# Folding U by f32 products on TensorE, and the rows of batch 0 half by half, in a kernel of two transforms and a mixer

## The chip, the cores and the metric

The kernel runs on one core of a Trainium2 chip. The metric is the device time of one execution in microseconds (us). The engines are TensorE (PE; its weight loads are PEld), VectorE (DVE), ScalarE (ACT), GpSimd (POOL) and SyncE (SP); DMA queues are issued from SP, ACT and POOL.

## The reference, cut to what matters

x is 8 x 3136 x 256 (batch, row, feature). The real part of its Fourier transform over rows and features is mixed over the rows by a low-rank pair U (3136 x 32) and V, and goes through two products with a ReLU between:

```
X = np.fft.fft(np.fft.fft(x, axis=1), axis=2).real
h = X.transpose(0, 2, 1) @ U @ V
u = X + h.transpose(0, 2, 1)
out = u + np.maximum(u @ w_ch1, 0) @ w_ch2
```

## The kernel before, in words

The transform over the 3136 rows is a product with tables of sines (`tabs`) and cosines (`tabc`), in bf16. The symmetry of the tables makes the work a quarter: rows n and S-n, and n and n+1568, are first added or subtracted. So batch b's rows come twice, `xf` forward (a gather on POOL, `load_f`, L67) and `xr` backward (`load_r`, L71; for batch 0 on SP), each in two halves a = 0 and 1 of 98 partitions x 8 rows x 256 features of f32 (784 KB), plus one-row edges (`load_0f`, `load_0r`). VectorE then folds. `along_d` (L299) folds along the features: part 0 subtracts (columns 1 to 127), part 1 adds (129 to 255). `alone` (L306, POOL) copies the two columns without a partner. `mirror` (L310) joins xf and xr of one half into `eos`, and `half` (L314) adds and subtracts the two halves into `G[b][par]`, the stationary operand of the row transform. `fold` (L318) is this for batches 1 to 7, `load_half` (L86) asks for the next batch's half once it has been read.

`seq` (L332) is one group of the row transform: 8 matmuls (4 for the later type) of 98 x 425 columns into a PSUM bank. Two groups of one parity and type are a pair: ACT copies the first to `ev` (L355), VectorE joins it with the second (L358 to L369) into `tab`, `A` and `B`. In batch 0 the order is g1, g2 (parity 0, type 0), g3, g4 (parity 1, type 0), g5 to g8 (type 1, on the later columns). Three banks serve all "dft" tiles, so g4 takes the bank of g1 and g6 that of g2. `chan` (L461) does the transform along the features from `A`, `B` with `MC`, `MSN`, `lowrank` (L472) the products with U, `front` (L504) the low-rank correction for 512 rows, `first_product` (L524) and `second_product` (L534) the two big products, 49 chunks of 512 rows. The fold and transform of the batches 1 to 7 are dealt out among these by `due` (L704 to L736).

U's own transform is columns 393 to 424 of the tables. For that U is folded in the same manner as x: UF is turned in its order of partitions by an f32 product with an exchange matrix `fl` (`turn_u`, L194), VectorE adds or subtracts UR from PSUM (L204) and then the halves (L207) into `GU` (`fold_u`, L202). `transform_u` (L222) contracts it with the tables on PE (L232), ACT keeps it (L238), PE turns it (L245), ACT writes it into the tables (L250, L251). `us` is this for the sines, `uc` for the cosines.

All of the set-up, batch 0's transform and the first chunk stand in an order written by hand (a manual schedule, from L93 until chunk 1): each engine does its instructions in the order of the program text. Lines 586 to 702 are that order. The tables' phases are on VectorE (`phase`, L167, two instructions each), their sines on ACT, mirrored copies on POOL or ACT (`turned_copy`, L264). The phases `pd` of the feature transform (L662 to L668) stand on VectorE between the fold of the first columns and that of the later ones; ACT makes `MSN` and `MC` of them, ahead of the first `ev` copy in its queue. The rows of batch 1 are asked for on POOL at L673 to L685.

Of the kernel before, what the change touches and what calls it, by code (L numbers as in the profile page):

```python
# [10 lines left out]
BF16 = mybir.dt.bfloat16  # L11
FP32 = mybir.dt.float32
I32 = mybir.dt.int32
# [14 lines left out]
def kernel(  # L28
# [81 lines left out]
    lrow = gen.tile([P, 2, P], FP32, tag="lrow", name="lrow", bufs=1)  # L110
    pcol = gen.tile([P, 1], FP32, tag="pcol", name="pcol", bufs=1)
    load_0f(moe_U, UF, 0, R, nc.scalar)
    load_0r(moe_U, UR, 0, R, nc.scalar)
    for t, n0, step in ((UF, 1, HALF), (UR, S - 784, -HALF)):
        nc.sync.dma_start(out=t[:PQ].rearrange("p a i d -> p a (i d)"),
                          in_=bass.AP(moe_U.tensor, moe_U.offset + n0 * R,
                                      [[8 * R, PQ], [step * R, 2], [1, 8 * R]]))
    load_r(0, 0)
    load_0f(x, xf, 0, D, nc.sync)
    load_0r(x, xr, 0, D, nc.sync)  # L120
    load_r(0, 1)
    for a in range(2):
        load_f(0, a)
# [1 line left out]
                   allow_small_or_imprecise_dtypes=True)  # L125
    nc.gpsimd.iota(fl[:, 1], pattern=[[1, P]], base=0, channel_multiplier=-1,
                   allow_small_or_imprecise_dtypes=True)
    nc.gpsimd.iota(fsel[:], pattern=[[R, 2], [2 * R, 2], [1, R]], base=0, channel_multiplier=-1,
                   allow_small_or_imprecise_dtypes=True)
    nc.gpsimd.iota(lrow[:], pattern=[[0, 2], [1, P]], base=0, channel_multiplier=0,  # L130
# [57 lines left out]
    uo = gen.tile([KP, 2, NI, R], FP32, name="uo", bufs=1)  # L188
    ue = gen.tile([KP, 2, NI, R], FP32, name="ue", bufs=1)
    GU = [gen.tile([KP, 2, NI, R], BF16, name=f"gu{par}", tag=f"gu{par}", bufs=1) for par in range(2)]  # L190

    TURNED = []

    def turn_u():  # L194
        nc.vector.tensor_single_scalar(fl[:], fl[:], 0.0, op=AL.is_equal)
        nc.vector.tensor_copy(fl[:KP, 0, PQ:KP], fl[:KP, 1, PQ:KP])
        pf = psum.tile([KP, 2, NI, R], FP32, tag="dft", name="pf", bufs=3)
        nc.tensor.matmul(pf.rearrange("p a i r -> p (a i r)"), fl[:KP, 0, :KP],
                         UF.rearrange("p a i r -> p (a i r)"), start=True, stop=True)
        TURNED.append(pf)  # L200

    def fold_u(typ):  # L202
        h = (uo, ue)[typ]
        nc.vector.tensor_tensor(h[:], TURNED[0][:], UR[:, :, ::-1, :],  # L204
                                op=AL.subtract if typ == 0 else AL.add)
        for par in range(2):
            nc.vector.tensor_tensor(GU[par][:, typ], h[:, 0], h[:, 1],  # L207
                                    op=AL.add if par == 0 else AL.subtract)


    hv = cpool.tile([P, 1], FP32, name="hv")
    hw = cpool.tile([P, 1], FP32, name="hw")
# [6 lines left out]
    def kp(i):  # L219
        return KP if i == NI - 1 else PQ  # L220

    def transform_u(typ):  # L222

        t = {}

        def contract():
            acc = t["acc"] = psum.tile([P, NQ], FP32, tag="dft", name="pu", bufs=3)
            for n in range(NI // 2):
                for g in range(4):
                    pk, pn = divmod(g, 2)  # L230
                    i = ktiles(pk)[n]
                    nc.tensor.matmul(acc[g * R:(g + 1) * R, :], GU[pn][:kp(i), typ, i, :],  # L232
                                     tabs[typ][:kp(i), i, pn, :NQ],
                                     start=(n == 0), stop=(n == NI // 2 - 1))
# [351 lines left out]
    for m, i in ((0, 0), (1, 2)):  # L586
        odd_row(m, i)
    cosine_odd(2)
    for m, i in ((2, 4), (3, 6)):
        odd_row(m, i)  # L590
    cosine_odd(6)
    for m, i in enumerate((7, 5, 3, 1)):
        phase(phe[:, m], krow[:KP, :, NH - 1:], ncol[:KP, i:i + 1], 15)
        sine(tabs[0][:, i, :, NH - 1:NQ], phe[:, m], 15, 1)
        if m == 0:
            mirror_even(0, 7)
            turn_u()
# [13 lines left out]
    fold_u(1)  # L611
    us, uc = transform_u(0), transform_u(1)
    us[0]()
    cosine(tabs[1][:, 7, :, NH - 1:NQ], phe[:, 0], 15)
    mirror_even(1, 7)
    cosine(tabs[1][:, 3, :, NH - 1:NQ], phe[:, 2], 15)
    nc.scalar.copy(cells(1, 3, 0, 1, NH - 1, 1), cells(1, 3, NQ - 1, -1, NH - 1, 0))
    us[1]()
    us[2]()
    cosine_low(5)  # L620
    cosine_high(1)
    us[3]()
    for a in range(2):
        alone(a, xr, EOR_)
    nc.gpsimd.iota(pint[:], pattern=[[0, 1]], base=D, channel_multiplier=-1)
    nc.gpsimd.memset(pint[0:1], P)
    nc.gpsimd.dma_start(out=W1[:, 0, :], in_=moe_w_ch1[0:P, :])
    w1t = gen.tile([P, H], FP32, name="w1t", tag="w1t", bufs=1)
    gather(w1t[:], moe_w_ch1, D, pint[:], H, 0)
    for a in range(2):  # L630
        alone(a, xf, EOF_)
# [3 lines left out]
    column_zeros()  # L635
    for s in range(2):
        nc.gpsimd.memset(TA[s][:].bitcast(I32), 0)
        if s == 0:
            av = alt.rearrange("p (l two) -> p l two", two=2)
            nc.gpsimd.memset(av[:, :, 0:1], 1.0)  # L640
            nc.gpsimd.memset(av[:, :, 1:2], -1.0)
        nc.gpsimd.tensor_copy(TA[s][R:R + 2, :], alt[R:R + 2, :])
        nc.gpsimd.memset(TA[s][R:R + 1, :], 0.0)
        nc.gpsimd.memset(TA[s][R:R + 1, 0:1], 1.0)
        nc.gpsimd.memset(TA[s][R:R + 1, P:P + 1], -1.0)
    for par in range(2):
        nc.gpsimd.memset(G[1][par][:, :, 258:GW].bitcast(I32), 0)
    along_d(0, xr, EOR_, 0)
    along_d(1, xr, EOR_, 0)
    halve(1)  # L650
    for step in uc:
        step()
    for a in range(2):
# [4 lines left out]
    for a in range(2):  # L658
        mirror(a, slice(256, 258), AL.add)
    for par in range(2):  # L660
        half(0, par, slice(256, 258))
    nc.vector.memset(lrow[:, 1, 0:1], 128.0)  # L662
    nc.vector.tensor_single_scalar(pcol[:], pcol[:], 1.0 / D, op=AL.mult)
    pd = gen.tile([P, 2 * P], I32, name="pd", bufs=1)
# [6 lines left out]
    for a in range(2):  # L671
        along_d(a, xr, EOR_, 1)
    for a in range(2):  # L673
        load_r(1, a)
    load_0r(x, xr, 1, D, nc.gpsimd)
    for a in range(2):
        along_d(a, xf, EOF_, 1)
        mirror(a, slice(128, 256), AL.add)
    for par in range(2):
        half(0, par, slice(128, 256))  # L680
    nc.gpsimd.memset(msr[:, :, 0:1], 1.0)
    nc.gpsimd.memset(msr[:, :, 1:2], -1.0)
    for a in range(2):
        load_f(1, a)
    load_0f(x, xf, 1, D, nc.gpsimd)  # L685
    nc.gpsimd.tensor_copy(W1[:, 1, :], w1t[:])
    nc.gpsimd.memset(VA[1][:].bitcast(I32), 0)
    nc.gpsimd.dma_start(out=VA[1][:R, :], in_=moe_V)
    steps = list(transform(0))
# [77 lines left out]
```

## Time and profile before

| what | before |
|---|---|
| three runs, median (lowest to highest) | 486.08 us (485.12 to 487.95) |
| the profiled execution: time, span | 486.03 us, 484.3 us |
| PE busy, share of the span | 459.6 us, 95% |
| VectorE busy | 317.0 us, 65% |
| ScalarE busy | 280.9 us, 58% |
| GpSimd busy | 69.1 us, 14% |
| mean granted clock of PE | 0.992 |
| PE idle before its matmuls of g1, from 24 us on | 2.43 us, released by VectorE's g |

The profile is of one execution. Its page gives busy times by engine, the busy tenths in 40 slices of the span, the chain of work that ended last, and groups of instructions by line; the timeline lists instructions in order of time, with the idle time of the engine before them and what ended it. Times in it count from the span's start. A busy PE is not a PE at its peak rate: matmuls of one shape take twice as long in some stretches as in others.

### The profile page before, as it was taken

The page shows a single profiled execution, that of the slowest core. Times are in us where ns is not written, and L with a number is a line of the kernel's source. Part 1 is how long each engine was busy: PE and PEld are TensorE (multiplying, and loading weights), DVE is VectorE, ACT ScalarE, POOL GpSimd, SP SyncE. Part 2 cuts the span into 40 slices and gives each one's busy share as a digit, 9 for nine tenths or more (in the row PEclk, how much of TensorE's full clock was granted, in tenths as well). Part 3 has the DMA queues.
Part 4 walks back from the last instruction along what each step waited for, and adds up shares of the span by engine and source line. Part 5 has one row for each costly group of instructions (what it writes and reads, how often), then busy time and mean ns, then how long its engine had stood idle before and what let it go on. Part 6 is the DMA issues. An engine that isn't in the chain of part 4 may idle for free.

```text
span 484.3 us, 7936 instructions
## 1 busy us (share of the span) xinstructions
PE 459.6 (95%) x3003; PEld 289.1 (60%) x3003; DVE 317.0 (65%) x713; ACT 280.9 (58%) x532; POOL 69.1 (14%) x123
## 2 busy tenths in 40 slices
PE   1479999999999999999999999999999999999997
PEld 0234656665566666666666666666666666666665
DVE  8895979684669657776568657684678543434333
ACT  7525744765666556655566556655566556656562
POOL 5882321110022000130022001120000000000000
PEclk9997999999999999999999999999999999999999
DMA  7589798975276823793376725684324233343533
GB/s 187 140 171 217 164 214 165 135 187 138 65 181 184 211 66 108 187 229 93 91 193 172 187 65 144 185 206 106 88 66 117 80 85 91 87 106 97 126 89 129
DMA packets 103606, 67.24 MB, mean 139 GB/s; under 512 B 73546, under 2 KB 100068, under 8 KB 100416
## 3 DMA queue, kind: packets, MB, share of 16 engines
q1 hardware_dynamic: 97722, 40.70, 36.4%
q0 software_dynamic: 5824, 26.03, 19.9%
q8 instruction: 23, 0.38, 0.3%
q14 instruction: 15, 0.12, 0.1%
q10 hardware_dynamic: 22, 0.00, 0.0%
HBM read 29.33 MB, written 25.69 MB: 114 GB/s over the span
## 4 chain that ended last, share of the span: by engine, by line
PE 87%; DVE 7%; DMA 3%; issue 1%; SPq 1%; DVEq 0%
PE p L546 34%; PE p L530 33%; PE pt L351 10%; PE ph L510 4%; DMA xr<-in_x_dram 3%; PE pst L466 2%; PE pst L468 2%; PE ptt L478 1%; DVE eof L304 1%; DVE eof L302 1%; DVE u L518 1%; DVE eos L311 1%; DVE eor L304 1%; PE ptc L437 1%; DVE eor L302 0%
## 5 line engine op out<-in xcount | busy, mean ns | idle before, releaser
L532 ACT ACTIVATE h<-p 128x512 bf16<-128x512 f32 x392 | 224.7, 599 | 153.8 <-PE p L530 153.7
L530 PE MATMUL p<-u,w 128*128 128x512 bf16 x784 | 218.3, 379 | 0.4 <-DVE u L518 0.3
L546 PE MATMUL p<-w,h 128*128 128x256 bf16 x1568 | 203.1, 273 | 0.0
L546 PEld LDWEIGHTS <-h 128*128 128x128 bf16 x1568 | 153.1, 98 | 59.4 <-DVE o L555 0.3
L530 PEld LDWEIGHTS <-w 128*128 128x128 bf16 x784 | 75.5, 98 | 53.6 <-issue 2.7
L552 DVE TENSOR_TENSOR o<-p,ut 128x4 f32<-128x4 f32 (+1 forms) x100 | 16.4, 164 | 93.1 <-PE p L546 91.2
L351 PEld LDWEIGHTS <-g 98*128 98x128 bf16 (+1 forms) x288 | 28.8, 101 | 34.0 <-DVE g L315 5.1
L358 DVE TENSOR_TENSOR tab<-pt,ev 128x32 bf16<-128x32 f32 x32 | 6.0, 189 | 58.2 <-PE pt L351 58.2
L55 POOL DMA_INDIRECT xf<-in_x_dram,xidx x16 | 17.3, 1079 | 170.2 <-DVE eof L304 162.9
L554 DVE TENSOR_TENSOR o<-p,ut 128x254 f32<-128x254 f32 (+1 forms) x100 | 40.5, 405 | 0.0
L555 DVE TENSOR_TENSOR o<-p,ut 128x254 f32<-128x254 f32 (+1 forms) x100 | 40.5, 405 | 0.0
L351 PE MATMUL pt<-tabc,g 98*128 98x425 bf16 (+1 forms) x160 | 37.9, 366 | 2.5 <-DVE g L315 1.7
L518 DVE TENSOR_TENSOR u<-ph,S 128x512 bf16<-128x512 f32 (+15 forms) x64 | 34.9, 554 | 2.1 <-ACT S L470 2.1
L518 DVE TENSOR_TENSOR u<-ph,T 128x512 bf16<-128x512 f32 (+15 forms) x64 | 34.8, 554 | 0.0
L351 PE MATMUL pt<-tabs,g 98*128 98x425 bf16 (+1 forms) x128 | 29.6, 355 | 2.4 <-DVE g L315 2.4
L510 PE MATMUL ph<-va,ta 128*128 128x512 bf16 (+18 forms) x128 | 29.4, 329 | 0.0
L355 ACT COPY ev<-pt 128x425 f32<-128x425 f32 x32 | 16.4, 514 | 22.4 <-PE pt L351 16.9
L311 DVE TENSOR_TENSOR eos<-eof,eor 99x1024 bf16<-99x1024 bf16 (+2 forms) x34 | 21.9, 660 | 0.1
L466 PE MATMUL pst<-A,mc 128*128 128x392 bf16 (+1 forms) x64 | 21.5, 335 | 0.2
L468 PE MATMUL pst<-B,msn 128*128 128x392 bf16 (+1 forms) x64 | 21.3, 333 | 0.0
L302 DVE TENSOR_TENSOR eor<-xr 99x1016 bf16<-99x1016 f32 x16 | 19.9, 1246 | 2.0 <-DMA xr<-in_x_dram 2.0
L315 DVE TENSOR_TENSOR g<-eos 99x2064 bf16<-99x2064 bf16 (+2 forms) x20 | 19.9, 1013 | 0.1
(130 smaller groups left out, 286.6 us busy)
## 6 DMA issues: line engine op xcount, KB each, us to landing
out_dram<-o SPq DMA_DIRECT2D x48, 512.0 KB
xr<-in_x_dram POOLq DMA_DIRECT2D x14, 784.0 KB, 6.8
xr<-in_x_dram SPq DMA_DIRECT2D x2, 784.0 KB
ut<-u SPq DMA_TRANSPOSE x49
w<-in_moe_w_ch_dram POOLq DMA_DIRECT2D x1, 512.0 KB, 8.4
out_dram<-o SPq DMA_DIRECT2D x4, 128.0 KB
va<-in_moe_V_dram POOLq DMA_DIRECT2D x2, 196.0 KB, 6.8
xf<-in_x_dram,xidx POOLq DMA_INDIRECT x16, 7.0
```

The lines of the kernel that those rows point to most:

```text
L302: pin(nc.vector.tensor_tensor(dst[:, a, :, 1:128], lo, hi, op=AL.subtract))
L311: pin(nc.vector.tensor_tensor(EOS[:, a, :, cols], EOF_[:, a, :, cols], EOR_[:, a, ::-1][:, :, cols], op=op))
L351: nc.tensor.matmul(pt[:], g[:kp(i), i, col:col + P], tabs[t][:kp(i), i, par, :], start=(n == 0), stop=(n == len(mm) - 1))
L466: nc.tensor.matmul(pt[:, :hi - lo], MC[:, h * P:(h + 1) * P], d["A"][:, lo:hi], start=True, stop=False)
L468: nc.tensor.matmul(pt[:, :hi - lo], MSN[:, h * P:(h + 1) * P], d["B"][:, lo:hi], start=False, stop=True)
L510: nc.tensor.matmul(ph[:, col:col + hi - lo], TA[b % 2][:, s * P:(s + 1) * P], VA[b % 2][:, lo:hi], start=True, stop=True)
L518: nc.vector.tensor_tensor(u[:, s, col:col + hi - lo], ph[:, col:col + hi - lo], src, op=AL.add)
L530: nc.tensor.matmul(p1[:], W1[:, s, j * P:(j + 1) * P], k["u"][:, s, :], start=(s == 0), stop=(s == 1))
L532: LAST[0] = nc.scalar.activation(k["h"][:, j, :], p1[:], AF.Relu)
L546: nc.tensor.matmul(p2[:, t % w, :], h[:, j, rs], W2[:, j, :], start=(j == 0), stop=(j == JT - 1))
L554: nc.vector.tensor_tensor(o[:, ts, 1:P], p2[:, :w, 1:P], ut[:, ts, 1:P], op=AL.add)
L555: nc.vector.tensor_tensor(o[:, ts, P + 1:D], p2[:, :w, P + 1:D], ut[:, tT, P - 1:0:-1], op=AL.add)
```

## The change

Three things are changed, all in the set-up and batch 0. First, U's fold is done by PE: for each type, parity and half the exchange matrix (for UF) or the unit matrix (for UR), with its sign, is multiplied with the rows in f32, four products of 256 columns summed in PSUM, eight for a type. `signs` makes the matrices and their negatives, and the two results are copied to `GU`, the first by VectorE, the second by ACT. `turn_u`, `uo` and `ue` go. Second, VectorE folds half 0 of batch 0 entirely (both parts, xr and xf, and their mirror) before it touches half 1. `halve(1)` and the transform of U's cosines stand between the two. The phases `pd` stand behind the fold of the later columns. Third, batch 1's rows are asked for by halves, as each is read, and the copies and zeros for TA, the columns and G[1] on POOL come later. Some small moves go with it: the one-row load of x's xr goes to ACT's queue and that of U's UR to SP's; a mirrored copy of the cosine table (row 7) goes from POOL to ACT, and the cosine of row 3 behind `us`'s first steps on ACT.

The diff, cut to its core:

```diff
-    load_0r(moe_U, UR, 0, R, nc.scalar)
+    load_0r(x, xr, 0, D, nc.scalar)
...
+    load_0r(moe_U, UR, 0, R, nc.sync)
     load_r(0, 0)
     load_0f(x, xf, 0, D, nc.sync)
-    load_0r(x, xr, 0, D, nc.sync)
     load_r(0, 1)
...
-    def turn_u():
+    def signs():
+        nc.vector.tensor_scalar(nfl[:], fl[:], 0.0, -1.0, op0=AL.is_equal, op1=AL.mult)
         nc.vector.tensor_single_scalar(fl[:], fl[:], 0.0, op=AL.is_equal)
-        nc.vector.tensor_copy(fl[:KP, 0, PQ:KP], fl[:KP, 1, PQ:KP])
-        pf = psum.tile([KP, 2, NI, R], FP32, tag="dft", name="pf", bufs=3)
-        nc.tensor.matmul(pf.rearrange("p a i r -> p (a i r)"), fl[:KP, 0, :KP],
-                         UF.rearrange("p a i r -> p (a i r)"), start=True, stop=True)
-        TURNED.append(pf)
-
-    def fold_u(typ):
-        h = (uo, ue)[typ]
-        nc.vector.tensor_tensor(h[:], TURNED[0][:], UR[:, :, ::-1, :],
-                                op=AL.subtract if typ == 0 else AL.add)
-        for par in range(2):
-            nc.vector.tensor_tensor(GU[par][:, typ], h[:, 0], h[:, 1],
-                                    op=AL.add if par == 0 else AL.subtract)
+        for t in (fl, nfl):
+            nc.vector.tensor_copy(t[:KP, 0, PQ:KP], t[:KP, 1, PQ:KP])
+
+    def fold_u(typ):
+        pf = psum.tile([KP, 2, NI, R], FP32, tag="dft", name="pf", bufs=3)
+        for par in range(2):
+            n = 0
+            for a in range(2):
+                sa = -1 if par == 1 and a == 1 else 1
+                for m, rows_, sgn in ((0, UF[:, a], sa),
+                                      (1, UR[:, a, ::-1], sa if typ == 1 else -sa)):
+                    nc.tensor.matmul(pf[:, par], (fl if sgn > 0 else nfl)[:KP, m, :KP], rows_,
+                                     start=(n == 0), stop=(n == 3))
+                    n += 1
+        return pf
...
-    for m, i in ((2, 4), (3, 6)):
-        odd_row(m, i)
+    odd_row(2, 4)
+    signs()
+    odd_row(3, 6)
     cosine_odd(6)
+    pf = [fold_u(0)]
...
-    fold_u(0)
     halve(0)
+    nc.vector.tensor_copy(GU[:, 0], pf[0][:])
+    pf.append(fold_u(1))
...
     us[0]()
     cosine(tabs[1][:, 7, :, NH - 1:NQ], phe[:, 0], 15)
-    mirror_even(1, 7)
+    nc.scalar.copy(cells(1, 7, 0, 1, NH - 1, 1), cells(1, 7, NQ - 1, -1, NH - 1, 0))
+    nc.scalar.copy(GU[:, 1], pf[1][:])
+    us[1]()
+    us[2]()
     cosine(tabs[1][:, 3, :, NH - 1:NQ], phe[:, 2], 15)
     nc.scalar.copy(cells(1, 3, 0, 1, NH - 1, 1), cells(1, 3, NQ - 1, -1, NH - 1, 0))
-    us[1]()
-    us[2]()
...
-    along_d(0, xr, EOR_, 0)
-    along_d(1, xr, EOR_, 0)
+    for part in range(2):
+        along_d(0, xr, EOR_, part)
+    along_d(0, xf, EOF_, 0)
+    mirror(0, slice(0, 128), AL.subtract)
+    along_d(0, xf, EOF_, 1)
+    mirror(0, slice(128, 258), AL.add)
     halve(1)
     for step in uc:
         step()
-    for a in range(2):
-        along_d(a, xf, EOF_, 0)
-        mirror(a, slice(0, 128), AL.subtract)
+    along_d(1, xr, EOR_, 0)
+    along_d(1, xf, EOF_, 0)
+    mirror(1, slice(0, 128), AL.subtract)
     for par in range(2):
         half(0, par, slice(0, 128))
...
+    load_r(1, 0)
+    load_f(1, 0)
+    along_d(1, xr, EOR_, 1)
+    load_r(1, 1)
...
+    ta_rows(0)
+    along_d(1, xf, EOF_, 1)
+    mirror(1, slice(128, 256), AL.add)
+    for par in range(2):
+        half(0, par, slice(128, 256))
     nc.vector.memset(lrow[:, 1, 0:1], 128.0)
     nc.vector.tensor_single_scalar(pcol[:], pcol[:], 1.0 / D, op=AL.mult)
...
+    load_f(1, 1)
+    load_0f(x, xf, 1, D, nc.gpsimd)
     load_0r(x, xr, 1, D, nc.gpsimd)
...
+    ta_rows(1)
+    column_zeros()
```

More of the change, by code (lines that the diff above doesn't have):

```diff
@@ L127 @@
                    allow_small_or_imprecise_dtypes=True)
+    nfl = gen.tile([P, 2, P], FP32, tag="nfl", name="nfl", bufs=1)
     nc.gpsimd.iota(fsel[:], pattern=[[R, 2], [2 * R, 2], [1, R]], base=0, channel_multiplier=-1,
@@ L187 @@
     phe = gen.tile([KP, NI // 2, 2, NH], I32, name="phe", bufs=1)
[L188 to L192, printed above, removed]
-    def turn_u():
+    GU = gen.tile([KP, 2, 2, NI, R], BF16, tag="gu", name="gu", bufs=1)
+    def signs():
+        nc.vector.tensor_scalar(nfl[:], fl[:], 0.0, -1.0, op0=AL.is_equal, op1=AL.mult)
         nc.vector.tensor_single_scalar(fl[:], fl[:], 0.0, op=AL.is_equal)
-        nc.vector.tensor_copy(fl[:KP, 0, PQ:KP], fl[:KP, 1, PQ:KP])
+        for t in (fl, nfl):
+            nc.vector.tensor_copy(t[:KP, 0, PQ:KP], t[:KP, 1, PQ:KP])
+    def fold_u(typ):
         pf = psum.tile([KP, 2, NI, R], FP32, tag="dft", name="pf", bufs=3)
-        nc.tensor.matmul(pf.rearrange("p a i r -> p (a i r)"), fl[:KP, 0, :KP],
-                         UF.rearrange("p a i r -> p (a i r)"), start=True, stop=True)
-        TURNED.append(pf)
-    def fold_u(typ):
-        h = (uo, ue)[typ]
-        nc.vector.tensor_tensor(h[:], TURNED[0][:], UR[:, :, ::-1, :],
-                                op=AL.subtract if typ == 0 else AL.add)
-        for par in range(2):
-            nc.vector.tensor_tensor(GU[par][:, typ], h[:, 0], h[:, 1],
-                                    op=AL.add if par == 0 else AL.subtract)
+        for par in range(2):
+            n = 0
[7 more added lines that the diff above has]
+        return pf
     hv = cpool.tile([P, 1], FP32, name="hv")
@@ L231, in contract @@
                     i = ktiles(pk)[n]
-                    nc.tensor.matmul(acc[g * R:(g + 1) * R, :], GU[pn][:kp(i), typ, i, :],
+                    nc.tensor.matmul(acc[g * R:(g + 1) * R, :], GU[:kp(i), typ, pn, i, :],
                                      tabs[typ][:kp(i), i, pn, :NQ],
@@ L596 @@
             mirror_even(0, 7)
-            turn_u()
         if i == 5:
@@ L606 @@
         cosine_odd(i)
-    fold_u(0)
     halve(0)
+    nc.vector.tensor_copy(GU[:, 0], pf[0][:])
+    pf.append(fold_u(1))
     nc.vector.tensor_single_scalar(sel.rearrange("p a c -> p (a c)"),
                                    fsel.rearrange("p a b r -> p (a b r)"), 0.0, op=AL.is_equal)
-    fold_u(1)
     us, uc = transform_u(0), transform_u(1)
@@ L622 @@
     us[3]()
-    for a in range(2):
-        alone(a, xr, EOR_)
+    alone(0, xr, EOR_)
+    alone(0, xf, EOF_)
     nc.gpsimd.iota(pint[:], pattern=[[0, 1]], base=D, channel_multiplier=-1)
     nc.gpsimd.memset(pint[0:1], P)
+    alone(1, xr, EOR_)
     nc.gpsimd.dma_start(out=W1[:, 0, :], in_=moe_w_ch1[0:P, :])
@@ L629 @@
     gather(w1t[:], moe_w_ch1, D, pint[:], H, 0)
-    for a in range(2):
-        alone(a, xf, EOF_)
+    alone(1, xf, EOF_)
     nc.gpsimd.memset(VA[0][:].bitcast(I32), 0)
@@ L634, with ta_rows @@
     nc.gpsimd.dma_start(out=W2[:], in_=moe_w_ch2.rearrange("(j p) d -> p j d", p=P))
-    column_zeros()
-    for s in range(2):
+    def ta_rows(s):
         nc.gpsimd.memset(TA[s][:].bitcast(I32), 0)
[L638 to L641, printed above, removed]
         nc.gpsimd.tensor_copy(TA[s][R:R + 2, :], alt[R:R + 2, :])
@@ L645 @@
         nc.gpsimd.memset(TA[s][R:R + 1, P:P + 1], -1.0)
-    for par in range(2):
-        nc.gpsimd.memset(G[1][par][:, :, 258:GW].bitcast(I32), 0)
-    along_d(0, xr, EOR_, 0)
-    along_d(1, xr, EOR_, 0)
+    for part in range(2):
[4 more added lines that the diff above has]
+    mirror(0, slice(128, 258), AL.add)
     halve(1)
@@ L652 @@
         step()
-    for a in range(2):
-        along_d(a, xf, EOF_, 0)
-        mirror(a, slice(0, 128), AL.subtract)
+    along_d(1, xr, EOR_, 0)
+    along_d(1, xf, EOF_, 0)
+    mirror(1, slice(0, 128), AL.subtract)
     for par in range(2):
         half(0, par, slice(0, 128))
-    for a in range(2):
-        mirror(a, slice(256, 258), AL.add)
+    mirror(1, slice(256, 258), AL.add)
     for par in range(2):
         half(0, par, slice(256, 258))
+    load_r(1, 0)
+    load_f(1, 0)
+    along_d(1, xr, EOR_, 1)
+    load_r(1, 1)
+    av = alt.rearrange("p (l two) -> p l two", two=2)
+    nc.gpsimd.memset(av[:, :, 0:1], 1.0)
+    nc.gpsimd.memset(av[:, :, 1:2], -1.0)
+    ta_rows(0)
[3 more added lines that the diff above has]
+        half(0, par, slice(128, 256))
     nc.vector.memset(lrow[:, 1, 0:1], 128.0)
@@ L670 @@
     MDT = [MSN, MC]
[L671 to L674, printed above, removed]
+    load_f(1, 1)
+    load_0f(x, xf, 1, D, nc.gpsimd)
     load_0r(x, xr, 1, D, nc.gpsimd)
[L676 to L680, printed above, removed]
     nc.gpsimd.memset(msr[:, :, 0:1], 1.0)
     nc.gpsimd.memset(msr[:, :, 1:2], -1.0)
-    for a in range(2):
-        load_f(1, a)
-    load_0f(x, xf, 1, D, nc.gpsimd)
     nc.gpsimd.tensor_copy(W1[:, 1, :], w1t[:])
+    ta_rows(1)
+    column_zeros()
+    for par in range(2):
+        nc.gpsimd.memset(G[1][par][:, :, 258:GW].bitcast(I32), 0)
     nc.gpsimd.memset(VA[1][:].bitcast(I32), 0)
```

## The prediction

> **What bounds the kernel now.** I read the page's slices first, then the chain that ended last, then the timeline of the first 47 us, engine by engine.
>
> The slices (each 12.1 us), PE and DVE:
> ```profile
> PE   1479999999999999999999999999999999999997
> DVE  8895979684669657776568657684678543434333
> ```
> PE is full from the fourth slice to the end. Only the first three have room, so a change to the set-up can only move the moment at which PE becomes full, and that shift is then carried to the end nearly one to one. The chain of waits says the same by line:
> ```profile
> PE p L546 34%; PE p L530 33%; PE pt L351 10%; PE ph L510 4%; DMA xr<-in_x_dram 3%; PE pst L466 2%; PE pst L468 2%; PE ptt L478 1%; DVE eof L304 1%; DVE eof L302 1%; DVE u L518 1%; DVE eos L311 1%; DVE eor L304 1%; PE ptc L437 1%; DVE eor L302 0%
> ```
> After the steady products (L546, L530) come a transfer of xr and VectorE's folds. The chain in order of time names where:
> ```profile
> 3.80 15.40 DMA xr<-in_x_dram
> ...
> 20.77 1.14 DVE eof L302
> ...
> 27.64 2.45 DVE eor L304 x2
> ...
> 36.49 4.44 PE pt L351 x12
> ```
> Timeline of that stretch (start, us, engine, line, operation, and in brackets the idle time before and who ended it):
> ```profile
> 8.99 2.00 PE L198 MATMUL pf<-uf,fl 99*99 99x512 f32 x2 [8.99 <-DVE fl L196]
> ...
> 15.43 1.84 DVE L302 TENSOR_TENSOR eor<-xr 99x1016 bf16<-99x1016 f32 x1
> ...
> 19.22 1.22 DVE L302 TENSOR_TENSOR eor<-xr 99x1016 bf16<-99x1016 f32 x1 [1.95 <-DMA xr<-in_x_dram]
> ...
> 25.31 1.60 PE L351 MATMUL pt<-tabs,g 98*128 98x425 bf16 x4 [2.43 <-DVE g L315]
> ...
> 27.30 0.34 DVE L171 TENSOR_SCALAR pd<-pd 128x256 int32<-128x256 int32 x1
> ...
> 28.80 0.51 ACT L183 ACTIVATE mc<-ab,c 128x256 bf16<-128x256 f32 x1
> ...
> 29.22 0.49 ACT L355 COPY ev<-pt 128x425 f32<-128x425 f32 x1
> ...
> 34.03 1.33 DVE L315 TENSOR_TENSOR g<-eos 99x1024 bf16<-99x1024 bf16 x2
> ...
> 34.81 0.90 PE L351 MATMUL pt<-tabc,g 98*128 98x425 bf16 x4 [1.67 <-DVE g L315]
> ...
> 35.86 0.58 DVE L369 TENSOR_TENSOR B<-pt,ev 128x392 bf16<-128x392 f32 x1
> ...
> 36.49 4.44 PE L351 MATMUL pt<-tabc,g 98*128 98x425 bf16 x12 [0.78 <-DVE B L369]
> ```
> VectorE waits 1.95 us for the second half of xr, although the first half had landed by 15.43. From 19.22 it is the bound: first half of the columns done at 25.77, the phases pd until 27.64, second half at 35.28. Batch 0's transform is eight groups of matmuls on PE, g1 to g8 (two each per parity and type, 8 matmuls each for g1 to g4, 4 for g5 to g8). g1 to g4 run from 25.31 to 33.14, g5 waits for the second half of the columns, and g6 for VectorE's reading of g2's bank.
>
> **The change part by part.**
>
> *U on PE.* Removed from DVE: the two f32 passes and four half passes of fold_u, 0.69 + 1.07 + 0.68 + 1.57 = 4.01 us (L204, L207). Added: the signs, two 128x256 compares (0.28 each, row L195) and two one-column copies (0.15), 0.85 us by the spacing of 8.42 to 8.74 to 8.81 against 0.39 before, and earlier by one phase pair; a copy of 99x512 out of PSUM (nearest row L204, 0.69). A second copy goes to ACT (nearest rows 0.49 at 425, 0.60 at 512 columns). Two memory-side moves (the one-row loads of U and x change queues) are 2 KB and 16 KB among 3.6 MB: nothing; they are covered by the bulk transfers.
>
> PE gets 16 f32 products of 256 columns for one of 512. The one took 2.00 us in two records that start 0.9 apart, with their weight loads (0.24 and 0.29) already lying beside it. So a 256-column product is half: 2 x 0.427 = 0.853 us in a stream at this rate, which is also that of bf16 there (four L351 of 425 columns in 1.42 us from 25.31, in 0.72 from 29.37: twice as fast). The rate rose 4.06 us after 25.31. Signs end at about 7.2 (third phase pair 6.49, plus 0.7), so products start at 7.25 if U has landed (bounds: before 8.99 and 11.03, when it is used now; by bytes, 0.40 MB at the head of a queue, when the windows of one us add up to 0.84 MB moved in all by 6.0). The eight products of the first type end at 14.35 at the low rate throughout; with the rate rising 4.06 us after 7.25, 4.8 products are done by 11.3 and 3.2 follow at 0.43, 12.95 with 0.25 of drain. DVE's phases end at 11.5, and it then waits: what is queued behind that copy is the whole fold of x. Copy and sel take 0.85, so DVE starts xr's first half at 13.8 to 15.2; I take 14.5 (15.43 if xr lands no earlier than we know). The gain against 15.43 is 0.9 us, not 4.
>
> The second eight products end at 16.35 (rate up) to 21.15 (never up). ACT takes row 7's mirrored copy from POOL (0.52, row L617) inside its wait for them. PE must then contract U and turn it, with ACT behind: GU copy, 0.55; three ops of the cosine, 1.75; two copies, 0.95; evictions. That ends the tables at about 24.7, or 28.6 at the worst; g1 needs VectorE's first columns (25.3) anyway.
>
> *Halves as they land.* From T0 = 14.5 DVE runs, by the rows above: xr half 0, both parts, 1.5 (beside POOL's copies, 1.84 alone there) + 1.2; xf part 0 and mirror 1.24 + 0.61; part 1 and mirror 1.35 + 0.73; halve 0.33; then half 1: 1.14 + 1.26 + 0.77; g 1.20. That is 10.75 to the first parity, 25.3 (25.2 before: first PE group unmoved), 11.33 to both. Then 0.33 of edge columns, 1.22 + 1.35 + 0.72, g 1.25: T0 + 16.2 = **30.7**, against 35.28. Half 1 is needed at 21.5, and landed at 19.2: that wait of 1.95 is gone.
>
> *What is late next.* The phases pd (1.33) now stand behind all this: they end at 32.0, not 27.64. ACT has msn, mc and only then g1's copy to ev in its queue. In the rows above this is 27.64 to 29.71, 2.07 us; so ev of g1 is done at 34.1 (29.71 before). Two things wait for it: g4, which takes g1's bank, so PE stands still from the end of g3 (31.7 by the old rows) until 34.1; and DVE's reading of g2 (1.16 us), which ends at 35.3 instead of 36.44. So of 4.6 us on VectorE, 1.15 reach that point, and 20 matmuls (g4 to g8) are still to come where 12 were. At the high rate they take 20 x 0.178 and some 0.8 of waits (g7 for ev of g5, g8 for g4's reading): g8 ends at 38.5, DVE's A at 39.2 where it was 41.73: 2.5 us won, and 0.25 more since the first products of L466 ran at the low rate until 42.6. At the low rate a matmul takes 0.355.
>
> Which rate? PEclk in the windows of one us:
> ```profile
> 35.00:36.00 1.00, 0.71 (x4) 0.19 (x2) 1.00 (x4) 0.00 (x0) 0.69 (x2) 1.00 0.88 344
> 36.00:37.00 1.00, 0.51 (x2) 0.28 (x3) 1.00 (x4) 0.45 (x1) 0.99 (x2) 0.50 0.95 262
> ```
> The last column but two falls from 1.00 to 0.50 at 36.0, after 2.45 us of idle time in 3.35. I expect 2.5 idle before g4. Bounds: no loss (0 us at the low rate), or the 6.1 us from 36.49 to the rise at 42.6. I take the other row, 4.06 us, the nearest to a start after a pause: low until 38.2, 11.4 matmuls by then, 8.6 more at 0.178, g8 at 39.75 instead of 40.93: 1.2 won, with the L466 term **1.5**. No loss gives 2.8; 6.1 us low gives 0.5.
>
> The Trainium skill ("TensorE: Matmul & The Clock Gate", Why this matters for your kernels) says that only idle gaps over about 3 us between bursts bring back the half rate; by that the estimate would be the 2.8. The drop here after 2.45 us in two pieces speaks against it.
>
> *Next rows by halves.* POOL asked for them at 31.9 to 36.4, and xf landed at 49.5 (POOL's copy of its edge had waited 9.3 us; DVE took it at 49.68). Now the first halves are asked at about 25, the last at 31: some 5 us earlier, while the front moves less. Cost nothing; were they as late as before, the whole gain would be lost there. TA, W1's cast and the zeros move behind them on POOL; W1's cast ended at 38.1 and would now end near 34.5, against first use at 46.3.
>
> *Sum.* The profiled execution took 486.03 (span 484.3 and 1.7 around it), the median is 486.08: 486.03 - 1.5 = **484.5**.
>
> **Rivals.**
> - *The rate is kept.* PE goes on at 0.178 a matmul behind the pause. For it: g5 started after a pause of 1.67 at the full rate. Against it: the drop at 36.0. 486.0 - 2.8 = 483.2.
> - *No gain.* T0 is 15.4 (xr lands late) and the low rate lasts 6.1 us: 485.9.
> - *Slower: the f32 products don't stream.* One instruction shows its second weight load hidden; between instructions with other weights nothing is shown. If each of the two loads is paid, a product takes 0.853 + 2 x 0.266 = 1.38 us, T0 comes 8 x 0.53 = 4.2 us later, and everything behind DVE with it: 484.5 + 4.2 = 488.7. The gain is gone from 0.96 to 1.04 us a product on. For it: DVE has nothing else to do while it waits. Against it: bf16 loads of L351 are hidden in full (0.355 x 1.2 = 425 columns).
>
> **How the numbers follow.** The forecast has 0.43, the kept rate 0.32, no gain 0.10, slower 0.15. The range leaves out most of the slower case and a little below: 482.0 to 488.0 (forecast's own: T0 from 13.8 to 15.4 and the rate, 482.9 to 485.9). A measurement here can tell 0.5% (2.4 us) from no change. Faster by more: two thirds of the kept rate and a quarter of the forecast, 0.32; slower 0.15; the rest 0.53.
>
> **What would show it.** In the profile after: f32 products of about 0.85 each from 7.3, then half that; DVE's first fold of xr at 14.5 and no wait for DMA behind it; second-half g ended at 30.7; pd at 32.0; ACT's first ev copy ended near 34.1 with PE idle until then; PEclk of 0.50 or 1.00 behind that; first L466 at 39 to 41. Wrong it would be if DVE stood past 15.4 at the copy of U, if g4 ran before the ev copy, or if DVE waited for rows of batch 1.

## The result and the profile after

Six runs of the changed kernel gave a median of 492.65 us (492.16 to 493.28); six of the kernel before gave 485.91 (485.01 to 487.95). The ratio is 1.0136, 95% interval 1.0114 to 1.0158: slower by 1.4%, where 484.5 was forecast. The profiled execution of after took 492.97 us with a span of 491.2, 6.94 more than that of before. Ratios here and below are taken over the executions within 1.5% of the fastest of their kernel: two of nine of e7 (491.4 and 491.5) and one of twelve each of e9 and e12 are left out, and what slowed those is not shown. In the transform and the chunks, lines of after are one higher than those of before (L466 is now L467, L530 is L531); in the set-up they differ by more.

The slices of after's page, PE, DVE and the granted clock:
```profile
PE   4683999999999999999999999999999999999997
DVE  8971797676677756786477657776569643344343
PEclk9877899999999999999999999999999999999999
```
PE is busier in the first two slices (the f32 products), but the fourth is now a gap (3 tenths), and the full stretch begins one slice later. The chain that ended last, in order of time, names a transfer there that before's chain did not have:
```profile
28.44 14.31 DMA xf<-in_x_dram,xidx
44.03 1.02 POOL xf L55
```
It is the gather of batch 1's rows, which batch 0 doesn't need. The timeline of POOL in after in that stretch (start, us, engine, line, operation; idle time before and its end in brackets):
```profile
28.44 1.46 POOL L55 DMA_INDIRECT xf<-in_x_dram,xidx  x1 [0.30 <-issue]
...
30.76 0.25 POOL L640 MEMSET ta<- 128x128 int32 x1
42.90 0.39 POOL L641 COPY ta<-alt 2x256 bf16<-2x256 bf16 x1 [11.89 <-DMA xf<-in_x_dram,xidx]
...
46.42 0.23 POOL L688 MEMSET msn<- 1x128 bf16 x1
```
The copy of two rows into TA, 0.39 us of work, stood 11.89 us until the gather that POOL had issued before it had landed. In before the copy stood ahead of batch 1's requests, with no idle time before it:
```profile
28.18 0.83 POOL L642 COPY ta<-alt 2x256 bf16<-2x256 bf16 x1
```
After's second such copy, at 50.16, likewise waited 2.26 us for the second gather. Behind the first one in POOL's queue stood batch 1's second gather and edge rows (44.03 to 46.2) and the alternating cells of `msn`'s first row (L687, L688), and PE needs these:
```profile
33.97 0.88 PE L352 MATMUL pt<-tabs,g 98*128 98x425 bf16 x4 [0.69 <-ACT ev L356]
34.69 3.87 PE L352 MATMUL pt<-tabc,g 98*128 98x425 bf16 x20
46.70 0.59 PE L479 MATMUL ptt<-msn,tab 128*32 128x256 bf16 x2 [8.14 <-POOL msn L688]
...
53.19 1.92 PE L531 MATMUL p<-u,w 128*128 128x512 bf16 x7
```
and in before:
```profile
46.30 1.92 PE L530 MATMUL p<-u,w 128*128 128x512 bf16 x8
```
Batch 0's transform ended at 38.56, 2.4 us ahead of before, and PE then stood 8.14 us. The first chunk's first product (L531) started at 53.19, in before at 46.30. These 6.89 us are the whole loss, within 0.05 of the 6.94. Of them, 5.83 are there when PE goes on (46.70, in before 40.87), and 1.06 come in the products from there to the first chunk, with a granted clock of 0.50 from 44 to 52 us (in before until 42.6).

Most of the change's own steps came out close to what was forecast; the time to the halving and PE's idle time before g4 did not, and the first product of L467 came late for the reason above:

| step | forecast | after |
|---|---|---|
| one f32 product of 256 columns, low and high rate | 0.853, 0.427 us | 0.855, 0.432 |
| rise of the rate | 4.06 us after 7.25 | about 4 us after 7.36 |
| VectorE starts xr | 14.5 (13.8 to 15.2) | 13.78 |
| from there to the cosine table's halving | 6.6 us | 7.88 |
| second-half g, pd, g1's ev copy end | 30.7, 32.0, 34.1 | 30.99, 31.85, 33.9 |
| PE idle before g4 | 2.4 us | 0.69 |
| g8 ends at the kept rate | 38.5 | 38.56 |
| first product of L467 | 39 to 41 | 47.65 |

None of the three signs by which the prediction said it would be wrong is in this profile: VectorE did not stand past 15.4 at the copy of U, g4 ran behind the ev copy, and VectorE waited for no rows of batch 1.

### The profile page after: what moved, and what is told of

It reads as the page before. It is cut to its first block, busy times and chain, and to the rows that moved or that the text cites. A ratio compares the mean times of both kernels' runs of the same rounds, so it can differ in the third digit from the quotient of the medians.

```text
span 491.2 us, 7944 instructions
## 1 busy us (share of the span) xinstructions
PE 462.7 (94%) x2979; PEld 295.3 (60%) x3033; DVE 314.4 (64%) x709; ACT 282.3 (57%) x534; POOL 70.2 (14%) x122
## 4 chain that ended last, share of the span: by engine, by line
PE 86%; DVE 5%; POOL 3%; DMA 3%; issue 2%; ACT 1%; DVEq 0%; POOLq 0%
PE p L547 34%; PE p L531 31%; PE pt L352 9%; PE ph L511 4%; DMA xf<-in_x_dram,xidx 3%; PE pst L467 3%; PE pst L469 2%; PE ptt L479 1%; PE ptc L438 1%; DVE u L519 1%; ACT tabs L177 1%; DVE pho L172 1%; POOL tabc L268 1%; DVE pho L170 0%; DVE eof L305 0%
## 5 line engine op out<-in xcount | busy, mean ns | idle before, releaser
L531 PE MATMUL p<-u,w 128*128 128x512 bf16 x732 | 208.5, 379 | 1.2 <-DVE u L519 0.3
L531 PEld LDWEIGHTS <-w 128*128 128x128 bf16 x784 | 75.5, 98 | 53.6 <-issue 2.7
L352 PEld LDWEIGHTS <-g 98*128 98x128 bf16 (+1 forms) x288 | 28.7, 100 | 30.8 <-issue 4.7
L519 DVE TENSOR_TENSOR u<-ph,S 128x512 bf16<-128x512 f32 (+15 forms) x64 | 34.9, 554 | 11.2 <-ACT T L471 11.2
L352 PE MATMUL pt<-tabc,g 98*128 98x425 bf16 (+1 forms) x160 | 36.2, 355 | 0.2
L511 PE MATMUL ph<-va,ta 128*128 128x512 bf16 (+13 forms) x126 | 29.3, 332 | 0.1
L356 ACT COPY ev<-pt 128x425 f32<-128x425 f32 x32 | 16.4, 515 | 16.6 <-PE pt L352 15.4
L467 PE MATMUL pst<-A,mc 128*128 128x392 bf16 (+1 forms) x64 | 22.3, 348 | 0.3
L303 DVE TENSOR_TENSOR eof<-xf 99x1016 bf16<-99x1016 f32 x16 | 19.9, 1244 | 0.0
```

The source lines that it names most:

```text
L303: pin(nc.vector.tensor_tensor(dst[:, a, :, 1:128], lo, hi, op=AL.subtract))
L352: nc.tensor.matmul(pt[:], g[:kp(i), i, col:col + P], tabs[t][:kp(i), i, par, :], start=(n == 0), stop=(n == len(mm) - 1))
L467: nc.tensor.matmul(pt[:, :hi - lo], MC[:, h * P:(h + 1) * P], d["A"][:, lo:hi], start=True, stop=False)
L511: nc.tensor.matmul(ph[:, col:col + hi - lo], TA[b % 2][:, s * P:(s + 1) * P], VA[b % 2][:, lo:hi], start=True, stop=True)
L519: nc.vector.tensor_tensor(u[:, s, col:col + hi - lo], ph[:, col:col + hi - lo], src, op=AL.add)
L531: nc.tensor.matmul(p1[:], W1[:, s, j * P:(j + 1) * P], k["u"][:, s, :], start=(s == 0), stop=(s == 1))
```

## The experiments

"First product" is PE's first instruction of the first chunk's first product, 46.30 in the profile of before.

**Is it the copy's wait?** Theory: the wait of the TA copy on the gathers, by their place in POOL's queue, is the loss. Rivals: the f32 products, the late pd, or the row requests themselves.

e1, the same copy over all 128 partitions (the extra rows meet zeros of VA); in this form it did not wait for the gathers:
```diff
-        nc.gpsimd.tensor_copy(TA[s][R:R + 2, :], alt[R:R + 2, :])
+        nc.gpsimd.tensor_copy(TA[s][:], alt[:])
```


> The changed kernel with one edit: the copy of alt into TA on POOL covers all 128 partitions instead of partitions 32 and 33 (the other rows are multiplied with zero rows of VA or overwritten), and as built it then waits for no transfer. Theory (POOL's wait at that copy for the gather of batch 1's xf, 30.98 to 42.90, is the whole loss): POOL goes on at 31, the one-row writes of MSN come at about 34, the products of lowrank start at about 38.6 instead of 46.70, the first product of L467 at 39.3 instead of 47.65, and the time falls by about 8 us, to 484 to 485. Rival (the f32 products or the new order of the fold are dear in themselves): the time stays at 491 or above. Rival (batch 1's rows, asked for late, hold the fold of batch 1): part of it stays, 487 to 490, with VectorE waiting for DMA.

Measured: 488.04 (486.38 to 489.24) beside 485.44 of before, ratio 1.0034 [1.0006, 1.0061]. The wait went, with some 4.6 us of the loss:
```profile
31.33 0.40 POOL L641 COPY ta<-alt 128x256 bf16<-128x256 bf16 x1
```
The first product was at 43.90, 2.4 us ahead of before. But the time is still not below before's. The timeline of e1 says where the rest went, first VectorE, then PE:
```profile
51.69 1.22 DVE L303 TENSOR_TENSOR eof<-xf 99x1016 bf16<-99x1016 f32 x1 [4.33 <-DMA xf<-in_x_dram]
```
```profile
58.94 0.39 PE L531 MATMUL p<-u,w 128*128 128x512 bf16 x1 [3.49 <-DVE u L519]
```
VectorE's fold of batch 1 now waits 4.33 us for the rows, and PE waits 3.49 us behind it. That is 3.5 of the 4.8 us that the profile of e1 loses behind the first product: it is 2.4 us ahead there, and its span is 2.4 us longer (486.7 against 484.3).

e2, both TA tables made ahead of the row requests:
```diff
+    ta_rows(0)
+    ta_rows(1)
     load_r(1, 0)
     load_f(1, 0)
     along_d(1, xr, EOR_, 1)
     load_r(1, 1)
-    ta_rows(0)
```


> The changed kernel with the alternating row and both TA tables made on POOL ahead of the first requests for batch 1's rows, two-partition copies as they were; the requests come some 3 us later. Theory (the wait behind the gather is the loss): as good as the run with the wide copy, 484 to 485, products of lowrank at about 39. Rival (asking early for the rows is what matters): slower than that run by the 3 us or so by which the rows come later.

Measured: 487.71 (486.03 to 491.06), ratio 1.0029 [1.0002, 1.0056]. The same as e1 by another way: order alone takes the wait off. In its profile, taken from its longest execution (491.06), VectorE waited 6.2 us for xf of batch 1 and PE 5.4 us for VectorE.

e3, the kernel before with its TA block moved behind the gathers of batch 1, nothing else:
```diff
     load_0f(x, xf, 1, D, nc.gpsimd)
     nc.gpsimd.tensor_copy(W1[:, 1, :], w1t[:])
+    for s in range(2):
+        nc.gpsimd.memset(TA[s][:].bitcast(I32), 0)
...
```


> The kernel before with only the alternating row and both TA tables moved on POOL behind its gathers of batch 1's rows (issued at 34.0 and 35.4, landed at about 49). Theory: the same wait appears without anything else of the change; front's first product (43.72) has to wait for TA until about 50, so 6 to 7 us are lost, 491 to 493. Rival (the wait hurts only together with the other moves): within 1 us of 486.

Measured: 495.03 (493.69 to 495.44), ratio 1.0157 [1.0102, 1.0212]. That move alone makes the old kernel slower by about as much as the whole change (the intervals overlap). In its table of waits (engine, line, what it waited for, us in total, times, longest) and in PE's timeline:
```profile
POOL ta L682 <- DMA xf<-in_x_dram,xidx: 11.2, 1, 11.2
```
```profile
50.04 1.03 PE L510 MATMUL ph<-va,ta 128*128 128x512 bf16 x2 [5.60 <-POOL ta L685]
```
The time was above the 491 to 493 forecast for it: here the gathers are asked later, the copy is released at 49.09, and the first product came at 55.08. So the wait goes with the place behind the gathers, and neither with the f32 products nor with the halves.

**What holds the rest?** Theory: the rows of batch 1 land too late for the earlier front. Rival: U's products or the late pd.

e4, e1 with U folded on VectorE as before:
```diff
-    pf = [fold_u(0)]
...
+            turn_u()
...
+    fold_u(0)
     halve(0)
-    nc.vector.tensor_copy(GU[:, 0], pf[0][:])
-    pf.append(fold_u(1))
+    fold_u(1)
```


> The kernel of the wide copy, with U's fold put back to VectorE and the single f32 product as before the change; the order of the rows by halves stays. Theory (the products on PE take 1.6 us off VectorE's start of the fold, 15.43 to 13.78, and all of it reaches the end): 1.5 us slower than the run with the wide copy, 485.5 to 486.5. Rival (PE's products bring nothing, since other waits end last): within 0.5 us of it. Rival (they delay the tables): faster by 0.5 us or more.

Measured: 487.45 (486.51 to 489.24), ratio 1.0032 [1.0004, 1.0059]: e1's time, although the first product was 1.65 us later (45.55). VectorE waited 1.2 us for the rows in place of 4.33.

e5, e1 with pd back between the column halves:
```diff
     for par in range(2):
         half(0, par, slice(256, 258))
+    phase(pd[:], lrow.rearrange("p a l -> p (a l)"), pcol[:], 17)
...
```


> The kernel of the wide copy, with the phases pd on VectorE put back between the first and the later columns, as before the change. In the wide-copy run ev of g1 ended at 34.3 and the first product of L467 stood at 39.8, 2 us ahead of the kernel before, yet VectorE then waited 4.3 us for batch 1's rows (landed 51.7, before 49.6), and PE 3.7 us for VectorE. Theory (the landing of batch 1's rows sets the end): the first product of L467 moves to about 37.5, VectorE's wait for the rows grows by as much, and the time stays within 1 us of 488. Rival (the chain of ev, g4 to g8 sets the end): 2 us faster, about 486.

Measured: 488.38 (488.03 to 489.04), ratio 1.0069 [1.005, 1.0088]. The first product was 1.34 us earlier (42.56), and nothing came of it:
```profile
51.92 1.22 DVE L303 TENSOR_TENSOR eof<-xf 99x1016 bf16<-99x1016 f32 x1 [5.91 <-DMA xf<-in_x_dram]
```
The earlier the front in e4, e1 and e5 (45.55, 43.90, 42.56), the later the fold of batch 1 (50.24, 51.69, 51.92): its rows end last. What ends VectorE's wait is the one-row edge behind the second gather on POOL, asked at 33.5 in e1 against 36.4 in before; the fold starts at 51.69 against 49.68. The queue of SP says what the rows now meet: two transposes for the first chunks, which start with the front. The first took 1.93, 1.66 and 1.75 us in before, e1 and e5. The second, in the same order:
```profile
49.78 1.23 SPq L521 DMA_TRANSPOSE ut<-u  x1
```
```profile
47.39 4.15 SPq L522 DMA_TRANSPOSE ut<-u  x1
```
```profile
46.05 5.64 SPq L522 DMA_TRANSPOSE ut<-u  x1
```
In before it ran when the rows had landed, in e1 and e5 beside them. It does not come from the early start alone: in e7 (below), where the rows land early, the second transpose started at 46.72 and took 1.23. The Trainium skill ("DMA: Bandwidth & Descriptors", Issuing engines are not separate DMA queues) says that transfers of all issuing engines run on the same 16 DMA engines and interleave. The trace agrees: a transpose issued from SP took 4.15 and 5.64 us in place of 1.23 while POOL's rows came, and the mean busy share of these engines (a sum of packet times, so it can pass 1) was 0.95 to 1.20 in e1 and e5 in each stretch of 5 us from 30 to 50, and 0.93 to 1.04 in before. That the transposes in turn delay the rows fits these times, but no run moves the transposes alone.

e8, e1 with batch 1's rows loaded for 49 of 98 partitions, so that half the rows of that batch are left out:
```diff
+        n = PQ // 2 if b == 1 else PQ
-        gather(xf[:PQ, a].rearrange("p i d -> p (i d)"), x, B * S // 8 - 1,
+        gather(xf[:n, a].rearrange("p i d -> p (i d)"), x, B * S // 8 - 1,
```


> The kernel of the wide copy, with batch 1's xf and xr loaded for 49 of the 98 partitions only, so that 1.6 of 3.2 MB are left out; batch 1 is then computed from rows of batch 0 in the other partitions. Nothing else moves. Theory (the landing of the rows): they land some 6 us earlier, VectorE waits for no row at 47, and the time is 484 to 485. Rival (something else than the transfers costs the 3 us): 487 to 488, as with all rows.

Measured: 485.39 (483.65 to 485.9), ratio 0.9997 [0.9982, 1.0012]. VectorE and PE no longer waited for rows (POOL's copy of the edge still did, until 46.94), and the time fell by 2.65 us against e1. In its profile the first product was also later than in e1 (45.76 against 43.90), so a part of the missing wait is the later front; that can't be what shortened the time.

e6, e1 with the backward rows and edges of batch 1 on SP's queue as each half is read, its first gather ahead of the weights on POOL, and its second gather right behind the last fold:
```diff
-        q = nc.sync if b == 0 else nc.gpsimd
+        q = nc.sync if b < 2 else nc.gpsimd
...
+    load_r(1, 0)
+    load_f(1, 0)
     nc.gpsimd.dma_start(out=W1[:, 0, :], in_=moe_w_ch1[0:P, :])
```


> The kernel of the wide copy, with batch 1's rows asked for earlier: xr and the one-row edges on SP's queue as soon as each half is read (about 20 and 28), the gather of xf's first half ahead of W1, w1t, V and W2 on POOL. Theory (the landing of the rows): they land by about 46, ahead of or early among the transposes of front, VectorE's wait of 4.3 us is gone, PE's of 3.7 with it: 484 to 485. Rival (the bytes are the bound whatever their order: W2 and V come late instead): PE waits for W2 or V, 487 to 489.

Measured: 486.18 (484.3 to 488.96), ratio 1.0031 [1.001, 1.0051]. The rows no longer hold VectorE (its fold of batch 1 starts at 47.26 without a wait), and its profiled execution took 485.15. In that one about 1.1 us went again near 108 us, where ACT waited 1.2 us for the late columns on SP's queue. The median is 1 us above it and did not get below before's; what holds it up is not shown.

e7, e6 and e5 together:

> Both edits together: batch 1's rows early, pd between the columns. Theory: with the rows there in time, the chain of ev and g4 to g8 counts again and 2 us more are won: 482 to 483. Rival (the transfers end last in any case): the same as with the rows early alone, within 0.7 us.

Measured: median 483.69, ratio 0.9961 [0.9948, 0.9975], below both kernels. The change with TA out of the gathers' way, early rows and early pd is worth 0.4%. That this comes from U on PE is not shown: e13 (below), with U on VectorE, has the same ratio.

e10, the kernel before with only batch 1's backward rows and edges on SP's queue:
```diff
-        q = nc.sync if b == 0 else nc.gpsimd
+        q = nc.sync if b < 2 else nc.gpsimd
```


> The kernel before, with only batch 1's backward rows and edges asked on SP's queue in place of POOL's. Theory: in the kernel before the rows of batch 1 land just as VectorE comes to them (49.5 landed, 49.68 taken, no wait recorded), so asking for them elsewhere gains nothing: within 0.5 us of 485.4, ratio 0.999 to 1.001. Rival: the rows are a bound in the kernel before too, and the 2 us of the last experiment come from them alone: 483.5 to 484, ratio 0.996.

Measured: 484.99, ratio 1.0001 [0.9977, 1.0025]. In the kernel before, earlier rows gain nothing that this interval shows; the rows become a bound when the front gets shorter (e1, e8).

e11, e7 with the column loads of the last stage asked closer together:
```diff
-        due.setdefault(8 + 5 * n // 4, []).append(step)
+        due.setdefault(8 + n, []).append(step)
```


> The version with early rows, early pd and U on PE, with the column loads for the last stage asked one a step in place of four in five steps, so that the last is asked some 8 us earlier. Theory: ACT's copy of those columns waited 1.1 us for the last load near 108 us and PE 1.1 us for ACT; with the loads earlier that wait goes, 482.6 where it was 483.7, ratio 0.993 to 0.995. Rival: the loads are held by the bytes that move there (rows of batch 2 and the transposes), so that asking earlier moves nothing, or takes bandwidth from the transposes: 483.5 to 484.5, ratio 0.996 to 0.998.

Measured: 489.15 (485.72 to 490.55), ratio 1.0075 [1.0045, 1.0105]. The wait for the columns went, but PE now waited 4.2 us in all for VectorE's u. The output chunk at 61.57 stood 6.94 us in SP's queue. The same stall came without denser loads in single executions of e7 (2.13 us near 107) and e13 (2.7 us), so what sets it off is left open.

**What is U on PE worth?** e9, e7 with U on VectorE:
```diff
-    pf = [fold_u(0)]
...
+    fold_u(0)
     halve(0)
...
+    fold_u(1)
```


> The kernel of the run before the last one (batch 1's rows asked early on SP's queue, the phases pd between the column halves, TA copied over all partitions) with U folded on VectorE as in the kernel before. Theory: U's products on PE win about 1.65 us of front (first product 43.9 against 45.55 in the pair with and without them), and they showed nothing at the end there only because the rows of batch 1 ended last. With the rows out of the way they should show: 1.65 us slower than the version with U on PE, 485.2 to 485.5 where that was 483.7, a ratio of 0.999 to 1.0015 to the kernel before. Rival: PE's products are worth nothing in any case (ACT's tables or VectorE's folds end last): 483.5 to 484, ratio 0.996.

Measured: 484.33, ratio 0.9995 [0.9969, 1.0022]. The ratio is the one expected, but its interval overlaps e7's, and the trace does not bear the reason out: the first product was at 43.26, in e7 at 43.23. VectorE did start x 1.29 us earlier in e7, and had lost it by the cosine table's halving (L257). VectorE in e7:
```profile
14.12 1.53 DVE L303 TENSOR_TENSOR eor<-xr 99x1016 bf16<-99x1016 f32 x1
15.57 1.52 DVE L305 TENSOR_TENSOR eor<-xr 99x1016 bf16<-99x1016 f32 x1
17.01 1.84 DVE L303 TENSOR_TENSOR eof<-xf 99x1016 bf16<-99x1016 f32 x1
18.89 1.21 DVE L312 TENSOR_TENSOR eos<-eof,eor 99x1024 bf16<-99x1024 bf16 x1
...
22.01 0.42 DVE L257 TENSOR_SCALAR tabc<-tabc,hv 99x786 bf16<-99x786 bf16 x1
```
and in e9:
```profile
15.41 1.84 DVE L303 TENSOR_TENSOR eor<-xr 99x1016 bf16<-99x1016 f32 x1
17.18 1.21 DVE L305 TENSOR_TENSOR eor<-xr 99x1016 bf16<-99x1016 f32 x1
18.32 1.22 DVE L303 TENSOR_TENSOR eof<-xf 99x1016 bf16<-99x1016 f32 x1
19.57 0.69 DVE L312 TENSOR_TENSOR eos<-eof,eor 99x1024 bf16<-99x1024 bf16 x1
...
22.11 0.42 DVE L257 TENSOR_SCALAR tabc<-tabc,hv 99x786 bf16<-99x786 bf16 x1
```
The same folds take 1.2 us or up to 1.84 us, the joining (`eos`) 0.69 or 1.21. This also corrects e4: of its 1.65 us of front, 1.30 are one such operation, the halving itself, which there took 1.72 us beside a copying POOL (the cast of L309) in place of 0.42; 0.21 are U.

e12 and e13, e7 and e9 with POOL's two large mirrored copies (tabc from tabs) ahead of its other copies:
```diff
     cosine_odd(6)
+    for i in (0, 4):
+        cosine_odd(i)
...
-    for i in (0, 4):
-        cosine_odd(i)
```


> The version with early rows, early pd and U on PE; POOL's two large mirrored copies (tabc from tabs, 99x784, 3.59 us from 16.0 on) stand ahead of its other copies, to run at about 8.5 to 11 beside VectorE's phases. Theory: U on PE lets VectorE start on x 1.3 us earlier (14.1 against 15.4), but beside these copies its folds of xr take 1.52 us in place of 1.2, the first of xf 1.84 and the first join 1.21 in place of 0.69, so that both versions are level at the cosine table's halving (22.01 and 22.11). With the copies gone from there the halving starts at 20.8 to 21.3 and the first product at 42.2 to 42.5 (43.23 before), 482.3 to 482.8 us. Rival: VectorE's folds are slowed by the row transfers that land at that time and not by POOL; then the halving stays at 22.0 and the front at 43.2, 483.5 to 484. The phases may take longer beside the copies; VectorE had 1.5 us to spare there.

> The same move in the version with U folded on VectorE. Theory: its folds of xr start at 15.4 and are hardly slowed (1.84, then 1.21 each), so the move gains 0.6 us on the first of them at most, and VectorE has no idle time ahead of them, so what the copies take from the phases (0 to 0.8 us) comes off again: halving at 21.5 to 22.5, first product 42.7 to 43.6, 483.5 to 485. With the run above this makes U's products on PE worth 0.5 to 1.2 us where the copies are out of the way, and 0.03 us where they are not. Rival: U's products are worth nothing in either case: both runs the same.

Measured: e12 484.21, ratio 0.9979 [0.9944, 1.0014]; e13 483.65, ratio 0.9961 [0.994, 0.9982]. The move did not do what the theory asked of it in e12: the copies slowed the signs and phases, VectorE started x at 15.64, and other copies of POOL then lay beside it; the halving was at 22.34, and 22.25 in e13. The first product was at 42.77 in e12 and 43.42 in e13, whose profile is of its longest execution (489.13). But the pair shows what goes with the longer folds, as both work on the same rows at the same time. VectorE and POOL in e12:
```profile
17.09 1.52 DVE L305 TENSOR_TENSOR eor<-xr 99x1016 bf16<-99x1016 f32 x1
```
```profile
16.16 1.38 POOL L268 COPY tabs<-tabs 99x392 bf16<-99x392 bf16 x1
17.49 1.23 POOL L309 CAST eor<-xr 99x16 bf16<-99x16 f32 x1
```
and in e13:
```profile
17.34 1.20 DVE L305 TENSOR_TENSOR eor<-xr 99x1016 bf16<-99x1016 f32 x1
```
```profile
18.71 1.07 POOL L309 CAST eor<-xr 99x16 bf16<-99x16 f32 x1 [2.13 <-DMA xr<-in_x_dram]
```
Where POOL copies, the fold takes 1.52 us, and the copy of 99x392 takes 1.38 in place of 0.51; where POOL waits, the fold takes 1.20. The f32 products that PE has in e12 alone are not the cause: in e9, without them, the fold at 15.41 took 1.84 beside POOL's copies (14.18 to 16.2). The Trainium skill ("SBUF — State Buffer", Who interferes with whom) has this rule: a VectorE instruction with two inputs in SBUF contends with a GpSimd instruction that reads SBUF. The trace agrees, with 1.52 against 1.20 us for the fold. What U's products on PE would be worth without the copies stays open; with them the two pairs (e7 and e9, e12 and e13) lean in opposite directions, and no gain can be told.

## Why the prediction was wrong

- **The step that failed.** "TA, W1's cast and the zeros move behind them on POOL" was priced by one due time (W1's cast, 38.1 to 34.5) and the last row request. The prediction did not list what POOL waits for at each moved instruction. The TA copy gained a wait of 11.89 us on a gather with which it shares no data, and `msn`'s cells behind it hold PE. e3 shows it alone (1.0157), e1 and e2 without it (1.0034, 1.0029). None of the three rivals had it.
- **"Next rows by halves ... Cost nothing"** also failed. The prediction gave the point itself: "were they as late as before, the whole gain would be lost there". The first halves were asked at 27.8 to 28.7 in e1 and the last at 32.5 to 34.1, where about 25 and 31 were forecast, and in after the last came at 44 to 46, behind the TA copy. With that wait gone, they were in later than before (51.7 against 49.7 in e1). That the front's earlier transposes take the same transfers fits the traces of e1 and e5; e8 shows that the rows are what costs. The prediction counted when the rows were asked, not what else would move then.
- **U on PE** was right in price and rate, and its start, 13.78, was the low end of the range. But the folds behind it were taken at their durations beside fewer copies: 7.88 us were needed where the terms up to the halving gave 6.6. Of the 1.64 us that VectorE started earlier, 0.45 were left at the halving (21.66, and 22.11 in e4).
- **A removed wait that is not in every run.** The 1.95 us for xr's second half were counted as gone. The wait is 2.18 us in the profile of e3, and absent in that of e10, whose program is the same up to there; e10's batch 0 ended at 39.22 in place of 40.93, its first product came at 44.74 in place of 46.30. So some 1.7 of the 2.4 us that after's batch 0 won against one profile of before may be no gain against its other executions.
- **The pd's place and the ev copy** were right within 0.3 us (31.85, 33.9).
- **The clock** went by the rival "the rate is kept", since PE's idle time before g4 was 0.69 us, not 2.4: the low rate had lasted to about 32, 6.0 us from g1's start (4.06 in before, about 4.1 in e10), so that g3 ended at 33.3 and not at 31.7; what sets this length stays open. The kept rate's 38.5 for g8 came out all the same (38.56). The 0.43 for a lost rate was a weak choice: the wait was worked out with g1 to g3 at the old rates.

## What to carry to other kernels

When an instruction is moved past a transfer that its own engine issues, look up what it waits for in the changed kernel, not only its inputs: here a copy of 0.39 us behind a gather waited 11.89 us for it, and everything behind it in the queue waited too. Ask for each stretch won in the front which transfers will now meet. A duration of VectorE read beside a copying POOL belongs to that pairing (1.52 us against 1.20 here): when one of the two moves, work the sum out with both values.

## What the runs showed that was not expected

- A POOL copy of two rows from partition 32 stood until the gather before it on POOL had landed (11.89 us in after, 11.2 in e3); the same copy over all 128 partitions did not. By the trace the wait ended with the landing of the gather, with which the copy shares no data. In e2, ahead of the requests, the two-row copies did not wait. Why the copy behind the gather is held is open.
- The second transpose of the front took 1.23 us where batch 1's rows had landed (before, e7), and 4.15 (e1) and 5.64 us (e5) beside them.
- PE kept its full rate after 0.69 us of idle time. After the 8.14 us the granted clock was 0.50 from 44 to 52 us. In before it had fallen to 0.50 after 2.45 us in two pieces (1.67 and 0.78).
